# Where the head layouts and the raw keys and queries stand among the loads of an attention and feed-forward kernel

## The chip, the cores and the metric

The kernel runs on one core of one Trainium2 chip. The time is device time in microseconds (us) of one execution. Runs of the same kernel are compared on the same chip; the kernel before has a median of 1001.68 us over 3 runs.

## The reference

Attention with pooled queries, and a feed-forward layer on its output, in float32:

```python
# q, k, v: (4, 8, 1152, 64); 32 heads in all
q_pool = q.reshape(B, H, S // 2, 2, D).mean(axis=3)
scores = scale * np.matmul(q_pool, k.transpose(0, 1, 3, 2))
scores = scores - np.max(scores, axis=-1, keepdims=True)
attn = np.exp(scores)
attn = attn / (np.sum(attn, axis=-1, keepdims=True) + 1e-09)
o = np.matmul(attn, v)
...
h = x @ w_in              # x: (2304, 512), w_in: (512, 2048)
r = np.maximum(h, 0.0)
g = s * (r * r) + b
return g @ w_out          # w_out: (2048, 512)
```

## The kernel before

Products that need more than one pass of a reduced format are split: a number is kept as a high part and the rest, and a product is summed from up to three matmuls. The 32 heads go in 16 pairs. A head takes 9 **steps**, one for each 128 keys, so a pair takes 18; `n` counts the steps and `n % 18` is the step of a pair. In a step TensorE (PE) makes the scores of one block (L486, four matmuls), the products of the block of three steps before with the values (`value_step`, L518 to L528), and one or two matmuls (L456) for the row maxima of a head that comes 15 steps later. ScalarE (ACT) makes the exponentials, VectorE (DVE) the maxima and part of the rests `pl`, GpSimd (POOL) the other rests `pl` (L501) and the preparation. After the attention (from about 585 us) the feed-forward part runs; the change does not touch it. In the last pairs of the attention, weights are converted too.

What is moved or waited for, by its step in a pair:

- `load_v` at steps 3 and 12 (L363): the values of the next head, 288 KB, into one of two buffers `vf`. Step 3 loads for the pair's second head.
- `prep_v` at steps 7 and 16 (L214, L431): POOL makes the high part `vv` and the rest `vl` out of `vf`. PE needs those of the second head from step 12 on.
- `load_k` and `load_q` at step `LR` (L350, L358): the raw keys and queries of the pair three ahead, 4 and 8 DMAs, in pieces of 128 bytes.
- the preparation of the pair two ahead, steps 9 to 14 (table `PREP`): POOL adds the queries (`qs`, L412), DVE transposes, POOL makes high parts and rests (`kh`, `kT`, `qh`, `qz`, `qT`).
- `lay(0)` and `lay(1)`, the entries `l0` and `l1` of `PREP` (L404 to L407): five DMAs inside the on-chip memory that put one prepared head into one of three buffers `kk`/`qq`, 1296 KB. The head is scored 14 steps or more later.
- `shift` (L468 to L472): once a head's maxima are done, DVE reduces them to `c`, and ACT sends `c` into `qq` by two small DMAs. For a pair's second head this is at the end of its step 2, for the first head of the next pair at the end of step 12.
- `xd<-xo` (L567) at step 10: a finished pair goes out.

All these but `c` are issued by SyncE (SP), in the order of the program. The framework gives each DMA of SP and of ACT one of eight completion counters in turn (`DMAHW0` to `DMAHW7`), in the order in which it lists the instructions of all engines. A DMA is issued only once the DMA that had its counter before has landed; the rows of the built program show this as a wait for `DMAHW`. In that list SP's DMAs stand later than the steps that call them, so a `c` that ACT sends can have a counter ahead of a DMA of SP that was called several steps before it.

The lines that decide the place:

```python
if p + 2 < NPAIR and n % 18 == PREP[0][1]:
    prep = prep_pair(p + 2)
for name, at in PREP if n >= 8 else ():
    if n % 18 == at and name in prep:
        prep.pop(name)()
if p + 2 < NPAIR:
    if n % 18 == LR and p + 3 < NPAIR:
        load_k(p + 3)
        load_q(p + 3)
```

Of the kernel before, what the change touches and what calls it, by code (L numbers as in the profile page):

```python
# [34 lines left out]
KIND = "vgvwvgvgw" * 2  # L35

PP = (("ka", 0), ("kb", 0), ("ha", 0), ("hb", 1), ("qs", 1), ("qt", 1), ("qm", 2), ("qh", 2), ("qz", 2), ("kl", 2), ("ql", 3), ("l0", 7))
PREP = (("qs", 9), ("ka", 10), ("kb", 11), ("ha", 11), ("qt", 12), ("hb", 12), ("kl", 12), ("qm", 13), ("qh", 13), ("qz", 13), ("ql", 14), ("l0", 0), ("l1", 8))
LR = 13
LD = 1  # L40
VS = (7, 16)
XT = (1, 2, 3, 4, 8)
# [10 lines left out]
def f32(ap):  # L53
    return ap.bitcast(F32)
# [3 lines left out]
def attention_moe_kernel(ctx: ExitStack, tc: tile.TileContext, q, k, v, w_in, w_out, s_in, b_in, out):  # L58
# [12 lines left out]
    NPAIR = NH // 2  # L71
# [138 lines left out]
    def hi_of(eng, out, in_):  # L210
        if eng is nc.scalar:
            nc.scalar.activation(out, in_, AF.Copy)  # L212
        else:
            eng.tensor_scalar(out=out, in0=in_, scalar1=1.0, scalar2=0.0, op0=ALU.mult, op1=ALU.add)  # L214
# [10 lines left out]
    def tick():  # L225
        step[0] += 1
        due = sorted(x for x in queue if x[0] <= step[0])
        queue[:] = [x for x in queue if x[0] > step[0]]
        for _, _, fn in due:
            fn()  # L230
# [99 lines left out]
    qm = ap.tile([P, P], F32R, name="qm")  # L330
# [16 lines left out]
    def load_k(p):  # L347
        kraw[p] = ap.tile([P, NB, 32], F32, tag="kraw", name=f"kraw{p}")
        for r, b, h, c in quarters(p):
            nc.sync.dma_start(kraw[p][r], k[b, h, :, c].rearrange("(j t) i -> t j i", t=32))  # L350
# [11 lines left out]
    def load_v(hd):  # L362
        nc.sync.dma_start(vfs[hd % 2][:, :, 0:D], v[hd // H, hd % H].rearrange("(j p) d -> p j d", p=P))  # L363

    def prep_pair(p):

        kr, qr = kraw.pop(p), qraw.pop(p)
        kT = ap.tile([P, S], F32, tag="kT", bufs=2, name=f"kT{p}")
        qT = ap.tile([P, SQ], F32, tag="qT", bufs=2, name=f"qT{p}")
        qs = ap.tile([P, NBQ, 32], F32, tag="qs", name=f"qs{p}")  # L370
        kh = ap.tile([P, S], F32R, tag="kh", bufs=2, name=f"kh{p}")
        qh = ap.tile([P, SQ], F32R, tag="qh", bufs=2, name=f"qh{p}")
        krv = kr.rearrange("p j i -> p (j i)")
        lo, hi = slice(0, SQ), slice(SQ, S)

        def corner():
            assert holds.get("qm", -1) == p - 1
            for h in range(2):
                d = slice(h * D, (h + 1) * D)
                hi_of(nc.scalar, qm[d, d], qT[d, NT4 * P:])  # L380
            holds["qm"] = p

        def k_hi(part, last):
            hi_of(nc.scalar if p < 2 else nc.gpsimd, kh[:, part], kT[:, part])
            if last:
                khs[p] = kh

        def q_hi():
            hi_of(nc.scalar if p < 2 else nc.gpsimd, qh, qT)
            qhs[p] = qh  # L390

        def q_blocks():

            for h in range(2):
                r = slice(h * D, (h + 1) * D)
                hi_of(nc.scalar if p < 2 else nc.gpsimd, qzs[p % 2][r, h].rearrange("p (t m) -> p t m", t=NT4), qT[r, :NT4 * P].rearrange("p (m t) -> p t m", t=NT4))

        def lay(h):
            hd = 2 * p + h
            kk, qq = kks[hd % 3], qqs[hd % 3].rearrange("p i a n -> p i (a n)")  # L400
            r = slice(h * D, (h + 1) * D)
            ks = ((f32(kk[D:P, 0, :]), kT[r]), (f32(kk[0:D]), f32(kh[r]).unsqueeze(1).to_broadcast([D, 2, S])))
            for dst, src in ks[::-1] if hd == 0 else ks:
                nc.sync.dma_start(dst, src)  # L404
            nc.sync.dma_start(f32(qq[0:D, 0, :]), f32(qh[r]))
            nc.sync.dma_start(f32(qq[D:P, 0, :]), f32(qh[r]))
            nc.sync.dma_start(f32(qq[0:D, 1, :]), qT[r])  # L407
            holds["k", hd % 3] = hd

        return {  # L410
            "ka": lambda: nc.vector.transpose(out=kT[:, lo], in_=krv[:, lo]),
            "qs": lambda: (nc.vector if p < 2 else nc.gpsimd).tensor_tensor(out=qs, in0=qr[:, :, 0, :], in1=qr[:, :, 1, :], op=ALU.add),  # L412
            "kb": lambda: nc.vector.transpose(out=kT[:, hi], in_=krv[:, hi]),
            "ha": lambda: k_hi(lo, False),
            "qt": lambda: nc.vector.transpose(out=qT, in_=qs.rearrange("p j i -> p (j i)")),
            "hb": lambda: k_hi(hi, True),
            "qh": q_hi,
            "qz": q_blocks,
            "kl": lambda: nc.gpsimd.tensor_tensor(out=kT, in0=kT, in1=f32(kh), op=ALU.subtract),  # L419
            "ql": lambda: nc.gpsimd.tensor_tensor(out=qT, in0=qT, in1=f32(qh), op=ALU.subtract),  # L420
            "qm": corner,
            "l0": lambda: lay(0),
            "l1": lambda: lay(1),
        }
# [55 lines left out]
    def score_step(hd, j, kind):  # L480
        assert holds["k", hd % 3] == holds["c", hd % 3] == hd
        kk, qq = kks[hd % 3], qqs[hd % 3]
        ps = ps_s.tile([P, 2, 512], F32, tag="s", name=f"s{hd}_{j}")
        for a in range(2):
            for i in range(2):
                nc.tensor.matmul(ps[:, a, :HALF], kk[:, i, j * P:(j + 1) * P], qq[:, i, a], start=(i == 0), stop=(i == 1))  # L486
        if kind != "v":
            pe = late.tile([P, 2, HALF], F32, tag="pe", bufs=PE, name=f"pe{hd}_{j}")
        if kind == "w":
            nc.scalar.activation(pe, ps[:, :, :HALF], AF.Exp, scale=SCALE)  # L490
            prob[hd, j] = pe, None
            return
        ph = late.tile([P, 2, HALF], F32R, tag="ph", bufs=PB, name=f"ph{hd}_{j}")
        pl = late.tile([P, 2, HALF], F32R, tag="pl", bufs=PB, name=f"pl{hd}_{j}")
        nc.scalar.activation(ph, ps[:, :, :HALF], AF.Exp, scale=SCALE)  # L495

        full = ps[:, :, :HALF] if kind == "v" else pe
        nc.scalar.activation(full, ps[:, :, :HALF], AF.Exp, scale=SCALE)  # L498
        prob[hd, j] = ph, pl
        eng = nc.vector if kind == "v" else nc.gpsimd  # L500
        fresh.append(lambda: eng.tensor_tensor(out=pl, in0=full, in1=f32(ph), op=ALU.subtract))  # L501
# [92 lines left out]
    prep = prep_pair(0)  # L594
# [11 lines left out]
    for n in range(AHEAD):  # L606
# [3 lines left out]
        if n == 11:  # L610
            load_v(1)
            prep = prep_pair(1)
    nc.sync.dma_start(sb[:, 0:1], s_in.unsqueeze(0).to_broadcast([P, 1]))
    nc.sync.dma_start(sb[:, 1:2], b_in.unsqueeze(0).to_broadcast([P, 1]))

    moe = Moe()
    weights_a = conversions(wa, wstage, 0, SW[0], 1, STA)
    NS = NH * NJ

    for n in range(NS + LAG):  # L620
        hd, j = divmod(n, NJ)

        at = (n - LAG) % NJ if n >= LAG else None
        products = None
        units = iter(range((n + AHEAD) * NU // 18, (n + AHEAD + 1) * NU // 18) if n + AHEAD < NS else ())
        for part in ORD[at] if at is not None else "sff":
            if part == "s" and n < NS:
                score_step(hd, j, KIND[n % 18])
            elif part == "f":
                for u in units:  # L630
                    max_unit(u, ps_m, "m")
                    break
            elif part == "v":
                if products is None:
                    products = value_step(*divmod(n - LAG, NJ))
                next(products)
        for fn in fresh:
            fn()
        fresh.clear()
        if n < NS:  # L640
            p, h = divmod(hd, 2)
            for name, at in PP:
                if n == at:
                    prep.pop(name)()
            if n == LD:
                load_k(2)
                load_q(2)
            if p + 2 < NPAIR and n % 18 == PREP[0][1]:
                prep = prep_pair(p + 2)
            for name, at in PREP if n >= 8 else ():  # L650
                if n % 18 == at and name in prep:
                    prep.pop(name)()
            if p + 2 < NPAIR:
                if n % 18 == LR and p + 3 < NPAIR:
                    load_k(p + 3)
                    load_q(p + 3)
            if hd + 1 < NH:
                if j == LAG and hd >= 1:
                    load_v(hd + 1)
                if n % 18 in VS:  # L660
                    prep_v(hd + 1)
            if n == NS - 3 * NJ:
                moe.fetch(0)
            if n == NS - 2 * NJ:
                moe.split(0, 1)
            if (CB - n) % CP == 0 and 0 <= CB - n < 7 * CP:
                weights_a()
        tick()
# [79 lines left out]
```

## Time and profile before

| | us |
|---|---|
| median of 3 runs | 1001.68 (998.31 to 1002.51) |
| profiled execution, its own time | 1000.3 |
| span in the profile | 998.4 |
| PE busy in the span | 921.4 (92%) |
| DVE, ACT, POOL busy | 630.1, 564.7, 549.8 |

The span is the time from the first to the last instruction in the profile; the 1.9 us around it belong to the execution's own time. PE is the busiest engine, and a busy PE is modelled from its starts, so what the kernel loses is read from PE's idle time and from what ended it.

### The profile page before, as it was taken

Reading aid. Unit: us, or ns where it says so; the run is one execution under the profiler, and the core shown is the slowest. Engines: PE = TensorE matmul, PEld = TensorE weight load, DVE = VectorE, ACT = ScalarE, POOL = GpSimd, SP = SyncE. Lnnn points to the kernel's source line nnn. Section 1 sums busy time; section 2 is a strip of 40 time slices with the busy share of each in tenths; the row PEclk is TensorE's granted clock in tenths of the full one; section 3 lists DMA queues with packets and bytes.
Section 4 is the critical chain, followed back from the end, with each engine's and each line's share of the span. In section 5 each row is a group of like instructions: output and inputs, shape, how many; then the busy total and the mean of one; then the engine's idle time right before and its main releaser. Section 6 shows DMA issues by size and latency. Waiting matters only on the chain.

```text
span 998.4 us, 16537 instructions
## 1 busy us (share of the span) xinstructions
PE 921.4 (92%) x5776; PEld 821.1 (82%) x5776; DVE 630.1 (63%) x1168; ACT 564.7 (57%) x1086; POOL 549.8 (55%) x437
## 2 busy tenths in 40 slices
PE   5998988899899899888889998999999999999998
PEld 3887877788788788877778887789999899999997
DVE  5766776676676668668767556676767664334333
ACT  2776665666676667667667856564444443333332
POOL 7667647757755785786695766673534440010000
PEclk9999999999999999999999999999999999999999
DMA  8987865865686597578574135665354433222311
GB/s 151 174 160 138 173 130 94 175 146 105 131 169 129 103 192 162 108 155 179 108 165 118 46 110 166 201 218 163 127 169 127 148 106 106 64 67 89 99 43 43
DMA packets 255313, 131.18 MB, mean 131 GB/s; under 512 B 203776, under 2 KB 227328, under 8 KB 255232
## 3 DMA queue, kind: packets, MB, share of 16 engines
q1 hardware_dynamic: 244512, 129.62, 54.4%
q10 hardware_dynamic: 10720, 0.52, 0.7%
q8 instruction: 46, 0.75, 0.3%
q14 instruction: 35, 0.29, 0.1%
HBM read 68.68 MB, written 18.87 MB: 88 GB/s over the span
## 4 chain that ended last, share of the span: by engine, by line
PE 58%; POOL 13%; DMA 8%; ACT 8%; DVE 6%; issue 4%; ACTq 1%; SPq 0%; POOLq 0%; DVEq 0%
PE h L272 16%; PE y L299 16%; PE s L486 9%; PE o L524 4%; PE m L456 4%; POOL pl L501 4%; PE o L528 4%; PE o L526 3%; PE o L518 3%; POOL kT L419 2%; POOL qz L214 2%; DMA vf<-in_v_dram 2%; DMA kk<-kh 2%; ACT ph L495 2%; DMA wsto<-in_moe_w_out_dram 2%
## 5 line engine op out<-in xcount | busy, mean ns | idle before, releaser
L457 DVE TENSOR_REDUCE pm<-m 128x1 f32<-128x384 f32 x432 | 233.0, 550 | 128.8 <-PE m L456 124.6
L495 ACT ACTIVATE ph<-s 128x576 fp32r<-128x576 f32 x224 | 145.9, 651 | 133.7 <-PE s L486 114.1
L272 PE MATMUL h<-x,wih 128*128 128x256 f32 x1152 | 213.2, 283 | 6.2 <-DVE gl L286 3.9
L486 PE MATMUL s<-qq,kk 128*128 128x288 f32 x1152 | 213.8, 308 | 4.1 <-DVE pl L501 3.6
L272 PEld LDWEIGHTS h<-x,wih 128*128 128x128 f32 x1152 | 185.8, 189 | 21.2 <-DVE gl L286 3.5
L501 POOL TENSOR_TENSOR pl<-pe,ph 128x576 fp32r<-128x576 f32 x96 | 137.5, 1432 | 104.8 <-ACT pe L498 103.5
L486 PEld LDWEIGHTS s<-qq,kk 128*128 128x128 f32 x1152 | 174.7, 192 | 16.4 <-PE o L528 4.4
L272 PE MATMUL h<-x,wil 128*128 128x256 f32 x576 | 162.2, 282 | 0.0
L528 PE MATMUL o<-pl,vv 128*128 128x288 f32 x448 | 135.7, 303 | 27.4 <-POOL pl L501 27.4
L456 PE MATMUL m<-kh,qz 128*128 128x384 f32 x384 | 153.5, 409 | 5.9 <-DVE pm L457 5.8
L524 PE MATMUL o<-ph,vv 128*128 128x288 f32 x448 | 138.7, 310 | 12.0 <-issue 4.4
L253 POOL TENSOR_TENSOR x<-xr,x 128x1024 fp32r<-128x1024 f32 x27 | 64.8, 2401 | 152.6 <-ACT x L212 146.9
L280 DVE SCALAR_TENSOR_TENSOR h<-h,sb,r 128x256 f32<-128x256 f32 x144 | 70.2, 488 | 115.2 <-ACT r L289 115.2
L526 PE MATMUL o<-ph,vl 128*64 128x288 f32 x448 | 134.1, 299 | 5.4 <-POOL vl L431 5.2
L528 PEld LDWEIGHTS o<-pl,vv 128*128 128x128 f32 x448 | 85.7, 191 | 45.9 <-POOL pl L501 35.4
L289 ACT ACTIVATE r<-h 128x256 f32<-128x256 f32 x144 | 55.7, 387 | 111.0 <-PE h L272 111.0
L501 DVE TENSOR_TENSOR pl<-s,ph 128x576 fp32r<-128x576 f32 x128 | 96.3, 752 | 28.5 <-ACT s L498 21.3
L299 PE MATMUL y<-wol,gh 128*128 128x512 f32 x288 | 113.1, 393 | 0.0
L299 PE MATMUL y<-woh,gl 128*128 128x512 f32 x288 | 112.9, 392 | 0.0
L299 PE MATMUL y<-woh,gh 128*128 128x512 f32 x288 | 112.6, 391 | 0.0
L272 PEld LDWEIGHTS h<-x,wil 128*128 128x128 f32 x576 | 109.6, 190 | 0.0
L524 PEld LDWEIGHTS o<-ph,vv 128*128 128x128 f32 x448 | 85.6, 191 | 25.1 <-ACT l L545 8.0
(89 smaller groups left out, 1492.0 us busy)
## 6 DMA issues: line engine op xcount, KB each, us to landing
kk<-kh SPq DMA_DIRECT2D x32, 576.0 KB, 5.6
kraw<-in_k_dram SPq DMA_DIRECT2D x64, 144.0 KB, 3.7
vf<-in_v_dram SPq DMA_DIRECT2D x32, 288.0 KB, 4.8
kk<-kT SPq DMA_DIRECT2D x32, 288.0 KB, 3.3
qq<-qh SPq DMA_DIRECT2D x64, 144.0 KB, 5.6
xr<-xd SPq DMA_DIRECT2D x18, 512.0 KB, 4.0
qraw<-in_q_dram SPq DMA_DIRECT2D x122, 72.0 KB, 2.5
wsti<-in_moe_w_in_dram SPq DMA_DIRECT2D x16, 512.0 KB, 5.0
```

The lines of the kernel that those rows point to most:

```text
L253: nc.gpsimd.tensor_tensor(out=xl, in0=xr, in1=f32(xh), op=ALU.subtract)
L272: nc.tensor.matmul(h[:, :TB], st[:, c, :], mv[:, c, :], start=(n == 0), stop=(n == 3 * NC - 1))
L280: nc.vector.scalar_tensor_tensor(out=t, in0=h[:, :TB], scalar=sb[:, 0:1], in1=r, op0=ALU.mult, op1=ALU.mult)
L299: nc.tensor.matmul(y[:, :DM], st[:, ts_], mv, start=(first and n == 0), stop=(last and n == 2))
L456: nc.tensor.matmul(ps[:, :KB], st, khs[p][:, e * KB:(e + 1) * KB], start=True, stop=True)
L457: nc.vector.tensor_reduce(out=pms[p][:, col, e:e + 1], in_=ps[:, :KB], axis=AX.X, op=ALU.max)
L486: nc.tensor.matmul(ps[:, a, :HALF], kk[:, i, j * P:(j + 1) * P], qq[:, i, a], start=(i == 0), stop=(i == 1))
L495: nc.scalar.activation(ph, ps[:, :, :HALF], AF.Exp, scale=SCALE)
L501: fresh.append(lambda: eng.tensor_tensor(out=pl, in0=full, in1=f32(ph), op=ALU.subtract))
L524: nc.tensor.matmul(o[:, :HALF], vv[:, j], ph[:, a], start=first, stop=False)
L526: nc.tensor.matmul(o[0:D, :HALF], vl[:, j], ph[:, a], start=False, stop=False)
L528: nc.tensor.matmul(o[:, :HALF], vv[:, j], pl[:, a], start=False, stop=last)
```

## The change

`l0` goes from step 0 of a pair to step 4, behind the value load of step 3; `l1` from step 8 to step 13, behind the value load of step 12; the raw keys and queries from step 13 to step 14, behind `l1`. So that `l1` can be called after `prep` has been replaced at step 9, the two entries are kept in a dictionary of their own, `lays`. The first pair's `l0` (table `PP`) stays.

```diff
-PREP = (("qs", 9), ("ka", 10), ("kb", 11), ("ha", 11), ("qt", 12), ("hb", 12), ("kl", 12), ("qm", 13), ("qh", 13), ("qz", 13), ("ql", 14), ("l0", 0), ("l1", 8))
-LR = 13
+PREP = (("qs", 9), ("ka", 10), ("kb", 11), ("ha", 11), ("qt", 12), ("hb", 12), ("kl", 12), ("qm", 13), ("qh", 13), ("qz", 13), ("ql", 14), ("l0", 4), ("l1", 13))
+LR = 14
...
+    lays = {}
...
-            if p + 2 < NPAIR and n % 18 == PREP[0][1]:
-                prep = prep_pair(p + 2)
-            for name, at in PREP if n >= 8 else ():
-                if n % 18 == at and name in prep:
-                    prep.pop(name)()
+            if n % 18 == PREP[0][1]:
+                lays = {k: prep[k] for k in ("l0", "l1") if k in prep}
+                prep = prep_pair(p + 2) if p + 2 < NPAIR else {}
+            for name, at in PREP:
+
+                ops = prep if name not in ("l0", "l1") or at < PREP[0][1] else lays
+                if n % 18 == at and name in ops and n >= 8:
+                    ops.pop(name)()
```

The first place is SP around the value load of step 3 (`vf1`), in the pair that scores heads 6 and 7. Before, from the fourth query DMA on (the number behind a name is that of a buffer; a wait for `DMAHWn` is one for the DMA that had counter n before):

```order
L358 DMA qraw5_1460<-in_q_dram 32x18x32 [waits DMAHW6_49]
L358 DMA qraw5_1460<-in_q_dram 32x18x32 [waits DMAHW7_49]
L358 DMA qraw5_1460<-in_q_dram 32x18x32 [waits DMAHW0_49]
L358 DMA qraw5_1460<-in_q_dram 32x18x32 [waits DMAHW1_49]
L358 DMA qraw5_1460<-in_q_dram 32x18x32 [waits DMAHW2_49]
L404 DMA kk2_96<-kT4_1348 64x1152 [waits DMAHW3_49,PE_49,Pool_49]
L404 DMA kk2_96<-kh4_1351 64x2x1152 [waits DMAHW4_49,PE_49]
L405 DMA qq2_99<-qh4_1352 64x576 [waits DMAHW5_49,Pool_49]
L406 DMA qq2_99<-qh4_1352 64x576 [waits DMAHW6_49]
L407 DMA qq2_99<-qT4_1349 64x576 [waits DMAHW7_49,Pool_49]
L363 DMA vf1_104<-in_v_dram 128x9x64 [waits DMAHW0_49,PE_49]
L404 DMA kk0_94<-kT4_1348 64x1152 [waits DMAHW1_49,PE_49]
```

Of these waits, the one for counter 0 in the third row and the one for counter 2 in the fifth (the sixth and the eighth query DMA) are waits for the two DMAs of `c7`, head 7's maxima. ACT sends `c7` at the end of step 2 of this pair; the query DMAs were called in step 13 of the pair before. In the changed kernel, from the fourth query DMA on:

```order
L358 DMA qraw5_1484<-in_q_dram 32x18x32 [waits DMAHW6_49]
L358 DMA qraw5_1484<-in_q_dram 32x18x32 [waits DMAHW7_49]
L358 DMA qraw5_1484<-in_q_dram 32x18x32 [waits DMAHW0_49]
L358 DMA qraw5_1484<-in_q_dram 32x18x32 [waits DMAHW1_49]
L358 DMA qraw5_1484<-in_q_dram 32x18x32 [waits DMAHW2_49]
L363 DMA vf1_104<-in_v_dram 128x9x64 [waits DMAHW3_49,PE_49]
L404 DMA kk2_96<-kT4_1343 64x1152 [waits DMAHW4_49,Pool_49]
L404 DMA kk2_96<-kh4_1346 64x2x1152 [waits DMAHW5_49]
L405 DMA qq2_99<-qh4_1347 64x576 [waits DMAHW6_49,Pool_49]
L406 DMA qq2_99<-qh4_1347 64x576 [waits DMAHW0_49]
```

Now `c7` has the counters 6 and 0, so the fourth and the sixth query DMA wait for it; the value load stands right behind the queries, and the five DMAs of `l0` behind it, without a wait for PE.

The second place is SP from the value load of step 12 (`vf0`) to the keys, in the pair that scores heads 4 and 5. Before:

```order
L404 DMA kk1_95<-kT3_921 64x1152 [waits DMAHW4_49,PE_49]
L404 DMA kk1_95<-kh3_924 64x2x1152 [waits DMAHW5_49,PE_49]
L405 DMA qq1_98<-qh3_925 64x576 [waits DMAHW6_49]
L406 DMA qq1_98<-qh3_925 64x576 [waits DMAHW0_49]
L407 DMA qq1_98<-qT3_922 64x576 [waits DMAHW1_49]
L567 DMA xd0_72<-xo1_1263 128x576 [waits DMAHW3_49,Pool_49]
L363 DMA vf0_103<-in_v_dram 128x9x64 [waits DMAHW4_49,PE_49]
L350 DMA kraw5_1455<-in_k_dram 32x36x32 [waits DMAHW5_49,DVE_49]
L350 DMA kraw5_1455<-in_k_dram 32x36x32 [waits DMAHW6_49]
L350 DMA kraw5_1455<-in_k_dram 32x36x32 [waits DMAHW7_49]
L350 DMA kraw5_1455<-in_k_dram 32x36x32 [waits DMAHW1_49]
```

The wait for counter 7, of the third key DMA, is the one for `c6` (head 6, sent at the end of step 12). In the changed kernel:

```order
L567 DMA xd0_72<-xo1_1263 128x576 [waits DMAHW6_49,Pool_49]
L363 DMA vf0_103<-in_v_dram 128x9x64 [waits DMAHW7_49,PE_49]
L404 DMA kk1_95<-kT3_916 64x1152 [waits DMAHW0_49]
L404 DMA kk1_95<-kh3_919 64x2x1152 [waits DMAHW1_49]
L405 DMA qq1_98<-qh3_920 64x576 [waits DMAHW2_49]
L406 DMA qq1_98<-qh3_920 64x576 [waits DMAHW3_49]
L407 DMA qq1_98<-qT3_917 64x576 [waits DMAHW4_49]
L350 DMA kraw5_1479<-in_k_dram 32x36x32 [waits DMAHW5_49,DVE_49]
L350 DMA kraw5_1479<-in_k_dram 32x36x32 [waits DMAHW7_49]
L350 DMA kraw5_1479<-in_k_dram 32x36x32 [waits DMAHW1_49]
L350 DMA kraw5_1479<-in_k_dram 32x36x32 [waits DMAHW2_49]
```

`l1` now stands between the value load and the keys. `c6` has the counters 2 and 5, so the third DMA of `l1` and the first key DMA wait for it. PE, ACT, DVE and POOL have the same work in the same order as before, but for the counters.

## Rows read from the trace of the kernel before

**Rows 1.** PE's waits, 70 to 350 us: total us, times, longest.

```profile
PE o L528 <- POOL pl L501: 18.3, 16, 1.6
PE o L526 <- POOL vl L431: 5.2, 6, 0.9
PE o L524 <- POOL vv L214: 4.0, 5, 1.5
```

**Rows 2.** PE's waits, 350 to 530 us.

```profile
PE o L528 <- POOL pl L501: 9.1, 7, 2.4
```

**Rows 3.** POOL's waits, 70 to 530 us.

```profile
POOL vv L214 <- DMA vf<-in_v_dram: 60.0, 13, 6.4
```

**Rows 4.** POOL in order of time: start, us, what, [idle before].

```profile
141.77 1.43 POOL L501 TENSOR_TENSOR pl<-pe,ph 128x576 fp32r<-128x576 f32 x1 [0.54 <-ACT pe L498]
149.57 0.67 POOL L214 TENSOR_SCALAR vv<-vf 128x576 fp32r<-128x576 f32 x1 [6.37 <-DMA vf<-in_v_dram]
...
161.46 1.40 POOL L501 TENSOR_TENSOR pl<-pe,ph 128x576 fp32r<-128x576 f32 x1
```

**Rows 5.** PE in order of time, the same stretch.

```profile
150.30 0.40 PE L524 MATMUL o<-ph,vv 128*128 128x288 f32 x1 [1.54 <-POOL vv L214]
...
151.78 0.35 PE L526 MATMUL o<-ph,vl 128*64 128x288 f32 x1 [0.91 <-POOL vl L431]
...
154.52 0.40 PE L528 MATMUL o<-pl,vv 128*128 128x288 f32 x1 [0.89 <-POOL pl L501]
...
162.91 0.40 PE L528 MATMUL o<-pl,vv 128*128 128x288 f32 x1 [1.61 <-POOL pl L501]
163.15 0.30 PE L524 MATMUL o<-ph,vv 128*128 128x288 f32 x1
```

**Rows 6.** SP in order of time: start, us over the group, what, count.

```profile
117.92 5.77 SPq L350 DMA_DIRECT2D kraw<-in_k_dram  x4
...
136.77 0.47 SPq L404 DMA_DIRECT2D kk<-kT  x1
...
142.48 0.61 SPq L363 DMA_DIRECT2D vf<-in_v_dram  x1
...
145.23 0.90 SPq L405 DMA_DIRECT2D qq<-qh  x1
...
149.66 0.60 SPq L567 DMA_DIRECT2D xd<-xo  x1
```

**Rows 7.** SP's own waits, 70 to 530 us.

```profile
SPq L358 <- DMA qq<-c: 119.0, 13, 11.5
```

**Rows 8.** ACT's issues of `c` (steps 2, 12, 2); landing of the first and second.

```profile
133.37 0.49 ACTq L471 DMA_DIRECT2D qq<-c  x1
...
151.71 0.49 ACTq L471 DMA_DIRECT2D qq<-c  x1
...
169.56 0.49 ACTq L471 DMA_DIRECT2D qq<-c  x1
...
qq<-c ACTq DMA_DIRECT2D x1, 2.0 KB, 1.9
...
qq<-c ACTq DMA_DIRECT2D x1, 2.0 KB, 4.7
```

**Rows 9.** Value loads to landing; query DMAs, ns each, and landing of five.

```profile
DMA to landing us min/median/max: 3.1/4.8/7.0
...
L358 SPq DMA_DIRECT2D qraw<-in_q_dram x122: 311/496/1522, 5.4 to 489.8; - x122
...
qraw<-in_q_dram SPq DMA_DIRECT2D x5, 72.0 KB, 2.4
```

**Rows 10.** A window: us, busy us of PE, PEld, DVE, ACT, POOL, PE's granted clock, DMA share, GB/s.

```profile
222.10:225.30 3.20, 3.03 (x13) 2.48 (x13) 2.09 (x3) 1.70 (x4) 3.12 (x5) 0.50 1.07 251
```

**Rows 11.** Windows of eight pairs and of the next five, columns as in Rows 10.

```profile
70.35:350.23 279.88, 248.96 (x1594) 221.94 (x1593) 191.05 (x345) 184.00 (x337) 187.42 (x154) 0.99 0.69 137
350.23:529.76 179.53, 161.21 (x1002) 142.18 (x1001) 130.82 (x234) 121.78 (x224) 132.62 (x109) 0.98 0.72 150
```

## The prediction

> **What bounds the kernel now.** I looked first for the idle time of the busiest engine. In the attention PE is busy 248.96 of 279.88 us over eight pairs (35.0 us a pair) and 161.21 of 179.53 us over the five pairs in which weights are converted as well (35.9 us a pair); DVE, ACT and POOL are each far less busy [rows 11]. So an unhindered PE would set the pace, and what the pairs lose is in PE's waits. Over the eight pairs it waits 18.3 us for rests `pl`, 5.2 us for `vl` and 4.0 us for `vv`, 27.5 us in all; over the five, 9.1 us for `pl` [rows 1, 2]. All of these POOL makes.
>
> The second view is POOL's own waits: it sits idle 60.0 us in 13 pairs, 4.6 us a pair, for the values `vf` [rows 3]. POOL works in order, so this one wait delays all that is queued behind it. In one pair it is done with the rest of step 7 at 143.20 us (141.77 and 1.43), waits 6.37 us, and begins `vv` at 149.57; the rest of step 14, 11.9 us of POOL's work later, begins at 161.46 and PE takes it at 162.91 [rows 4, 5]. PE's four waits of that pair (1.54, 0.91, 0.89, 1.61) hang on the one load [rows 5].
>
> The third view, SP in order of time, tells why the load is late. It was called at step 3 but issued at 142.48, after the keys, the queries and `l0`, which alone holds SP from 136.77 to 142.48, 5.7 us [rows 6]. And the queries did not go out as fast as SP could: SP waits 119.0 us, in 13 pairs, with a query DMA for the landing of a `c`, 9.2 us each [rows 7]. The rows of the built program, in the section on the change, show why: the sixth query DMA has a counter that the `c` of step 2 had before it. In this pair ACT sends `c` at 133.37, and it lands 1.9 us later [rows 8]. I call 133.37 the pair's zero: `c` lands at 1.9, the load is issued at 9.1, `vv` begins at 16.2, and POOL was free for it at 9.8.
>
> **The change, part by part.** It removes no work and adds none: the same DMAs, the same instructions on every engine.
>
> *Behind the wait.* Before, three queries (0.5 us each [rows 9]) and `l0` (5.7 us) stood between the landing of `c` and the load: 7.2 us. Now the fourth query has `c`'s counter, so five queries stand there, 2.5 us, and `l0` comes after the load. The load is issued at 4.4 if `c` lands in 1.9 us, at 7.2 if it lands in 4.7, as the one of step 12 does with keys in flight [rows 8]. Value loads take 3.1 to 7.0 us to land, 4.8 in the median [rows 9]. Today a layout stands ahead of the load; then it is queries, which land in 2.4 us [rows 9]. I bound the landing by 3.1 and by 3.1 + 2.4 = 5.5, and take 4.0. The values are there at 4.4 + 3.1 = 7.5 at best and at 7.2 + 5.5 = 12.7 at worst; with `c` landing in 3.3 us, midway since keys will be draining, at 5.8 + 4.0 = 9.8. POOL is free at 9.8 too. So POOL's wait goes nearly to nothing. A rule of the Trainium skill speaks against it: by "DMA: Bandwidth & Descriptors" ("Specifications") pieces under 512 bytes miss the line rate, and the load now stands behind five DMAs of 128-byte pieces. By the rule the load would land at the late end, and the sum would be that of the first rival below; no run here shows yet what a load behind queries takes.
>
> *Does the wait of PE go with it?* PE reaches the rest of step 14 at 162.91; without its four waits, and 0.1 us for each restart (a first product takes 0.40 us and not 0.30), it would be there at 162.91 - 4.95 - 0.4 = 157.6 [rows 5]. POOL, begun at 143.20, has that rest done 11.9 + 1.40 us later, at 156.5 [rows 4]. That is 1.1 us in hand: the wait can go, but a POOL that begins over 1 us late makes PE wait again.
>
> *The moved layouts.* `l0` now follows the load, and `l1` the load of step 12. Neither waits for PE any more, since the buffer is long free. They are needed 14 steps later, some 27 us at 1.9 us a step, for a few us of transfer: nothing. If that cover were gone, scores would wait.
>
> *The raw keys and queries* go behind `l1`, and they wait for `c` of step 12 with `l1`'s third DMA. From that `c`, sent at 151.71, to the next at 169.56 there are 17.8 us, of which the two later waits of PE take 2.7; in 15.1 us SP gets 4.7 for the landing, 4.4 for the rest of `l1` (145.23 to 149.66), 5.8 for the keys and 1.5 for three queries: 16.4 [rows 5, 6, 8]. The next `c` then lands at 15.1 + 1.9 to 4.7, so SP is ready 0.6 to 3.4 us before it. It fits, but not by much. POOL adds the queries only behind `vv` and `vl`, so not before 9.8 + 0.67; the last ones are issued by 7.2 and land 2.4 us later.
>
> *The sum.* PE's waits on POOL: 27.5 + 9.1 = 36.6 us in 34 waits [rows 1, 2], and 3.4 us of restarts, 40.0. Off that: a POOL that begins late now and then, which I put at 0.5 us of PE in each of 13 pairs, 6.5; and half of the 9.1 in the five pairs with weights, where POOL has 26.5 us of work a pair and not 23.4 [rows 11], 4.6. On to that: the clock. In a window of 3.2 us the granted clock is 0.50, that is 1.2 GHz instead of 2.4 [rows 10], and the mean over the two stretches is 0.99 and 0.98 [rows 11]: up to 0.01 x 279.88 + 0.02 x 179.53 = 6.4 us, if it fell for PE's waits. I take 2.4, since the means are rounded and the cause is open. "TensorE: Matmul & The Clock Gate" of the Trainium skill ("The HAM clock gate") calls the throttled state the default, which activity releases; by it all 6.4 would come back if the waits go, and the sum would be 4.0 lower.
>
> 40.0 - 6.5 - 4.6 + 2.4 = 31.3 us. The profiled execution took 1000.3 us, so I predict 969.0. That execution lies 1.4 us under the median, 1001.68, which changes nothing here.
>
> **The rivals.**
>
> *The load stays late (0.12).* `c` lands among the keys in 4.7 us and the load behind the queries takes 5.5: the values are there at 12.7 and POOL waits 2.9 us a pair instead of 4.6. For it speaks the rule above, and that SP reaches the fourth query only just in time; against it, that a longer pair gives SP the time back. It leaves 37% of 40.0, 14.8 us: 985.5.
>
> *POOL's second half becomes the bound (0.13).* The load comes in time, but the 1.1 us in hand are eaten by work that today hides in the wait: half of the 18.3 us and all of the 9.1 for `pl` stay, 18.3, with 1.5 of restarts. Then 40.0 - 19.8 = 20.2: 980.1. For it speaks that POOL's 11.9 us have no idle time between them.
>
> *Slower (0.03).* The raw loads behind `l1` overrun. SP must be ready for the fourth query before `c` lands; each us beyond the 0.6 to 3.4 in hand makes the values later, and from 16.2, instead of 9.8, the load is later than before. So it decides from an overrun of 6.4 us on top of the margin; one of 7.8 us would cost 1.4 us in 13 pairs, 18: 1018. The rest of `l1` and the keys take 4.4 and 5.8 us today [rows 6], and they would have to take nearly double.
>
> *No change that shows (0.03).* PE's waits go, but the maxima or the exponentials take their place. DVE and ACT are busy 68% and 66% [rows 11], so this needs a queue that I don't see: 998.
>
> **How the numbers follow.** My forecast has the remaining 0.69. Its own range is 956 to 980: the low end is all of the 40.0 and most of the clock, the high end doubles the two terms that I took off. With the first two rivals 0.94 lies on the faster side. Leaving out the slow cases and the tail of the late load, 80% is 955 to 984. The measurement can tell about 0.5%, 5 us, from no change: faster by more 0.94, within it 0.03, slower 0.03.
>
> **What the profile after would show.** SP: the load of step 3 right behind the eight queries, 4.4 to 7.2 us after `c`, and `l0` behind it; the wait of the queries for `c` still there, but shorter. POOL: `vv<-vf` waits at most 10 us in place of 60. PE: no waits for `vv` and `vl`, those for `pl` under 13 us over both stretches, and a pair of about 32 us. I am wrong if POOL's wait stays over 30 us, if `pl` waits stay with POOL never idle, or if scores wait for `kk` or `qq`.

## The result, and the profile after

The changed kernel takes 990.5 us in the median (989.04 to 991.4, 4 runs), the kernel before 1000.86 beside it (998.31 to 1002.51, 4 runs): a ratio of 0.9897, 95% interval 0.9871 to 0.9923. It is faster by 10.4 us, where 31 were forecast, and lies outside the range of 955 to 984. The profiled execution took 989.98 us, its span is 988.0.

The waits show first that the predicted thing happened. POOL's wait for the values, from 70 to 515 us (total us, times, longest):

```profile
POOL vv L214 <- DMA vf<-in_v_dram: 2.8, 5, 0.8
```

This was 60.0 us in 13 pairs [rows 3]. SP in order of time, in the pair of [rows 6], and POOL under it:

```profile
134.95 2.48 SPq L358 DMA_DIRECT2D qraw<-in_q_dram  x5
137.52 0.44 SPq L363 DMA_DIRECT2D vf<-in_v_dram  x1
138.06 0.77 SPq L404 DMA_DIRECT2D kk<-kT  x1
...
147.75 0.38 SPq L363 DMA_DIRECT2D vf<-in_v_dram  x1
148.18 0.60 SPq L404 DMA_DIRECT2D kk<-kT  x1
148.83 0.62 SPq L404 DMA_DIRECT2D kk<-kh  x1
```

```profile
142.85 0.67 POOL L214 TENSOR_SCALAR vv<-vf 128x576 fp32r<-128x576 f32 x1
143.60 1.44 POOL L431 TENSOR_TENSOR vl<-vf,vv 128x576 fp32r<-128x576 f32 x1
```

The load goes out right behind the queries and ahead of `l0`, at 137.52 instead of 142.48 [rows 6], and POOL begins `vv` without a wait, at 142.85 instead of 149.57 [rows 4]. PE's waits in eight pairs (68 to 345 us), and in the five behind them (345 to 515):

```profile
PE s L486 <- DVE pl L501: 16.5, 8, 2.3
...
PE o L528 <- POOL pl L501: 1.9, 4, 0.6
```

The first row is from the eight pairs, the second from the five. PE's waits for POOL's rests and values are nearly gone: 27.5 and 9.1 us before [rows 1, 2], 0.4 and 1.9 now. But in each of the eight pairs PE now waits about 2 us, with the next scores `s`, for a rest `pl` that DVE makes. One such wait, followed back: PE, then DVE, then ACT, each in order of time:

```profile
150.12 0.81 PE L486 MATMUL s<-qq,kk 128*128 128x288 f32 x4
...
153.26 0.29 PE L528 MATMUL o<-pl,vv 128*128 128x288 f32 x1
155.50 0.77 PE L486 MATMUL s<-qq,kk 128*128 128x288 f32 x4 [1.94 <-DVE pl L501]
```

```profile
150.22 0.17 DVE L468 TENSOR_REDUCE c<-pm 128x5 fp32r<-128x15 f32 x1
...
151.27 0.56 DVE L457 TENSOR_REDUCE pm<-m 128x1 f32<-128x384 f32 x1 [0.19 <-PE m L456]
154.60 0.76 DVE L501 TENSOR_TENSOR pl<-s,ph 128x576 fp32r<-128x576 f32 x1 [2.77 <-ACT s L498]
```

```profile
149.41 0.65 ACT L490 ACTIVATE pe<-s 128x576 f32<-128x576 f32 x1
150.42 0.49 ACTq L471 DMA_DIRECT2D qq<-c  x1
151.00 2.32 ACTq L472 DMA_DIRECT2D qq<-c  x1
153.37 0.65 ACT L495 ACTIVATE ph<-s 128x576 fp32r<-128x576 f32 x1 [3.31 <-PE m L456]
153.92 0.65 ACT L498 ACTIVATE s<-s 128x576 f32<-128x576 f32 x1
```

DVE is not busy; it waits 2.77 us for ACT. ACT is not busy either. Its exponential at 153.37 shows a wait of 3.31 us put down to PE, but the scores that it reads were done at 150.93 (L486, 150.12 and 0.81). What stands directly ahead of it is ACT's own queue: 0.4 us until DVE has made `c`, 0.5 for the first DMA of the step-12 `c`, and 2.32 us in which the second (L472) is being issued. Just ahead, at 148.18 and 148.83, SP has issued the two large DMAs of `l1`. That line over 68 to 345 us (duration in ns, minimum, median and maximum), before and then after:

```profile
L472 ACTq DMA_DIRECT2D qq<-c x16: 474/613/1027, 81.8 to 344.3; - x16
```

```profile
L472 ACTq DMA_DIRECT2D qq<-c x16: 613/1448/2692, 82.3 to 337.7; - x16
```

In the changed kernel the eight of step 12 take 2.28 to 2.69 us each, the eight of step 2, which have no layout ahead of them, 0.61. No counter holds the eight: the DMAs that each of them has to wait for, by the counters, had landed 9.4 us or more before its issue began. SP's own rows have the same hold, before the change too. The fourth DMA of a layout, the second small one behind the two large ones (L406), before and then after:

```profile
138.84 2.64 SPq L406 DMA_DIRECT2D qq<-qh  x1
...
146.18 2.57 SPq L406 DMA_DIRECT2D qq<-qh  x1
```

```profile
140.45 2.66 SPq L406 DMA_DIRECT2D qq<-qh  x1
```

Before, it took 2.43 to 2.69 us in all sixteen layouts of the eight pairs. In the changed kernel it takes 2.44 to 2.78 in `l0` and 0.60 in `l1`, where the two DMAs of `c` go out between the large ones and SP's small ones. The hold has gone from SP, where no exponential stood behind it, to ACT.

The last thing to read is the clock. Windows of the eight pairs, the five, the pair behind them and a short one behind one of the waits (columns as in [rows 10]):

```profile
70.84:343.58 272.74, 251.84 (x1594) 225.75 (x1593) 189.48 (x345) 183.74 (x336) 188.24 (x153) 0.98 0.68 140
343.58:515.45 171.87, 158.44 (x1003) 139.40 (x1002) 133.52 (x234) 121.66 (x225) 134.94 (x109) 1.00 0.73 156
515.45:551.88 36.43, 31.99 (x197) 28.63 (x196) 22.53 (x39) 24.95 (x45) 20.68 (x16) 0.95 0.40 105
120.90:124.30 3.40, 3.40 (x12) 2.83 (x12) 1.61 (x3) 1.61 (x3) 2.77 (x2) 0.50 0.44 103
```

Over the eight pairs PE's idle time fell from 30.92 to 20.90 us, and its busy time rose by 2.9, against [rows 11], so that 7.1 us are gained. In the window at 120.90 the granted clock is 0.50, that is 1.2 GHz; PE had waited 2.15 us just before it. The same comes behind waits of 2.31, 2.26 and 2.13 us; the others, of 1.9 to 2.0 us, have none behind them. (The length of the wait doesn't decide it alone: in the run below with the two DMAs of `c` in the other order, a clock of 0.50 stands behind waits of 1.79, 1.86 and 1.99 us, and none behind one of 2.13.) The five pairs gain 7.7 us. The pair behind them loses 3.6 (32.85 us before): it has the new wait, 2.13 us, and a slow clock behind it. That makes 11.2 us; the rest of the span gives 0.8 of them back, and 10.4 remain.

### The profile page after: what moved, and what is told of

The parts are those of the page before. It is cut to its first block, busy times and chain, and to the rows that moved or that the text cites. A ratio compares the mean times of both kernels' runs of the same rounds, so it can differ in the third digit from the quotient of the medians.

```text
span 988.0 us, 16507 instructions
## 1 busy us (share of the span) xinstructions
PE 921.8 (93%) x5776; PEld 822.9 (83%) x5776; DVE 631.3 (64%) x1168; ACT 564.2 (57%) x1086; POOL 552.7 (56%) x437
## 4 chain that ended last, share of the span: by engine, by line
PE 63%; DVE 9%; ACT 9%; POOL 6%; DMA 6%; issue 3%; ACTq 3%; SPq 1%; DVEq 0%; POOLq 0%
PE h L272 18%; PE y L299 17%; PE s L486 10%; PE m L456 4%; PE o L524 4%; PE o L528 4%; PE o L526 3%; PE o L518 3%; DVE pm L457 2%; ACT ph L495 2%; DVE pl L501 2%; ACTq L472 2%; DMA wsto<-in_moe_w_out_dram 2%; ACT s L498 2%; POOL pl L501 2%
## 5 line engine op out<-in xcount | busy, mean ns | idle before, releaser
L486 PE MATMUL s<-qq,kk 128*128 128x288 f32 x1152 | 215.6, 310 | 24.9 <-DVE pl L501 24.2
L486 PEld LDWEIGHTS s<-qq,kk 128*128 128x128 f32 x1152 | 174.5, 192 | 40.7 <-issue 23.7
L528 PE MATMUL o<-pl,vv 128*128 128x288 f32 x448 | 133.1, 297 | 1.9 <-POOL pl L501 1.9
L501 DVE TENSOR_TENSOR pl<-s,ph 128x576 fp32r<-128x576 f32 x128 | 96.2, 751 | 50.7 <-ACT s L498 49.0
L283 ACT ACTIVATE gh<-h,sb 128x256 fp32r<-128x256 f32 x144 | 68.1, 473 | 64.6 <-DVE h L280 64.3
```

What stands on the lines that cost most here:

```text
L283: nc.scalar.activation(gh, t, AF.Identity, bias=sb[:, 1:2])
L528: nc.tensor.matmul(o[:, :HALF], vv[:, j], pl[:, a], start=False, stop=last)
```

## The experiments

**Theory A**: the two large DMAs of `l1`, which SP now issues just ahead of the step-12 `c`, hold ACT's second DMA of that `c`, and with it the exponentials, DVE's rest and PE. **Theory B**: DVE's transposes crowd together at steps 10 to 12, and DVE is late by itself. The first four kernels ran beside a median before of 1000.62 us, the next four beside 1000.51, the last two beside 1001.53; the kernel before differs by 1 us between the groups, so kernels of different groups are compared by their times. "Wait" is PE's wait for `pl` from DVE from 68 to 345 us, 16.5 us in the changed kernel.

**Only `l0` moved.** `l1` is back at step 8:

```diff
-... ("l0", 4), ("l1", 13))
-LR = 14
+... ("l0", 4), ("l1", 8))
+LR = 13
```

> The layout of the first head at step 4 as in the change, that of the second back at step 8 and the raw loads at step 13. Theory A (the second layout's two large DMAs, issued just ahead of the step-12 maxima c, hold ACT's second c DMA for 2.3 us, so that exponentials, DVE's rests and then PE come late): here the layout is issued several us before c, ACT's second c DMA takes 0.6 us again, PE's wait for DVE's pl (16.5 us in eight pairs) goes under 3 us, and the time is 965 to 972 us. Theory B (with POOL no longer waiting, DVE's transposes fall together at steps 10 to 12 and make its rests late): the wait of PE stays as in the changed kernel and the time is 988 to 993 us.

971.01 us, ratio 0.9708 (0.9687 to 0.9728). One half of the change is thus worth 29.6 us, and the other half takes 19.5 of them back.

```profile
PE s L486 <- DVE pl L501: 3.7, 9, 0.9
...
L472 ACTq DMA_DIRECT2D qq<-c x17: 558/613/1273, 80.9 to 335.4; - x17
```

No second DMA takes over 1.27 us, the wait falls to 3.7 (A had under 3), and from 34 us to the last microsecond no stretch has a clock of 0.50. DVE's transposes are at the same steps as in the changed kernel. B falls.

**Only `l1` moved.** `l0` is back at step 0:

```diff
-... ("l0", 4), ("l1", 13))
+... ("l0", 0), ("l1", 13))
```

> The layout of the second head at step 13 and the raw loads at 14 as in the change, that of the first head back at step 0, ahead of the value load of step 3. Both theories: POOL waits for the values again, 50 to 65 us in 13 pairs, so the gain is gone. Theory A: ACT's c DMA is held where the layout is close ahead of it, which adds up to 1 us a pair: 1000 to 1010 us. Theory B: POOL is late as in the kernel before, so DVE is not crowded: 998 to 1002 us.

994.4 us, ratio 0.994 (0.992 to 0.996): faster, where both theories had no change or a loss, so A missed here too. POOL still waits 50.7 us for the values, and ACT's second DMA is held 2.22 to 2.53 us at each step-12 `c`. But PE's wait for DVE is 9.7 us and not 16.5. Over both stretches it is 17.8 instead of 2.0 before, and the waits for POOL's rests are 10.3 instead of 27.4. The two do not add up: while PE stands for DVE, POOL catches up, and the wait that would have come next is gone. That is how I read the rows; no run tested it.

**The `c` of the first head two steps later**, everything else as changed:

```diff
-        later(1, send)
+        later(1 if h else 3, send)
```

> The changed kernel with the maxima c of a pair's first head sent two steps later (end of step 14 and not 12), the second head's as before. Theory A: by then the layout's large DMAs have been worked off for 3 us more, the hold on ACT falls below 1 us, PE's wait for DVE's pl falls under 5 us in eight pairs, and the time is 966 to 976 us. Theory B: 988 to 993 us, since DVE's work does not move.

962.22 us, ratio 0.9622 (0.9602 to 0.9642), the fastest kernel here that does all the work, and a little under A's range. There is no wait for DVE left in the eight pairs, and the mean clock is 0.998. Windows of its eight and five pairs:

```profile
70.03:320.55 250.52, 245.94 (x1594) 221.86 (x1593) 189.31 (x345) 183.80 (x336) 188.39 (x153) 1.00 0.75 152
320.55:490.92 170.37, 157.90 (x1003) 139.45 (x1002) 132.00 (x234) 121.65 (x225) 134.17 (x109) 1.00 0.74 157
```

The second DMA of those `c` still takes 0.97 to 1.68 us, and PE does not wait for it. ACT shows why:

```profile
145.59 0.49 ACTq L471 DMA_DIRECT2D qq<-c  x1
145.79 0.65 ACT L495 ACTIVATE ph<-s 128x576 fp32r<-128x576 f32 x1
146.12 1.35 ACTq L472 DMA_DIRECT2D qq<-c  x1
146.34 0.65 ACT L498 ACTIVATE pe<-s 128x576 f32<-128x576 f32 x1
147.57 0.65 ACT L495 ACTIVATE ph<-s 128x576 fp32r<-128x576 f32 x1 [0.58 <-PE s L486]
```

Exponentials still run while the DMA is being issued, so that ACT sits idle for 0.28 to 0.93 us ahead of the next one, and not for 3.27 to 3.68 as in the changed kernel. The fourth DMA of `l1` is SP's again, and takes 2.43 to 2.67 us there.

**One DMA of the `c` left out.** The first head of each pair but the first pair doesn't get its second DMA, so the maxima of its last 64 queries aren't updated:

```diff
+            if h or hd < 2:
                 nc.scalar.dma_start(f32(row[D:D + 1, NT4 * P:]), ...)
```

> The changed kernel without the second of the two c DMAs of each pair's first head (but the very first): the maxima of the last 64 query rows of these heads are not brought up to date, all other work stays. Theory A: nothing is left on ACT to be held but the first c DMA, which was not held (0.49 us), so PE's wait for DVE's pl falls under 3 us in eight pairs: 965 to 972 us. Theory B: 988 to 993 us.

961.0 us, ratio 0.9607 (0.959 to 0.9624), 4 us under A's range. `l1` is where the change put it, the first DMA of that `c` is issued where it was, and the wait is gone. So the 29.5 us between this kernel and the changed one hang on that DMA of 64 words a pair: on its hold and on the half microsecond that it takes without one. (With one DMA fewer, the counters of all the later ones shift too.)

**The later `c` alone**, in the kernel before (the edit of one line above):

> The kernel before with one edit: the first head's c is sent two steps later; no layout and no load is moved. Theory A (the two large DMAs of l1 just ahead of the c of step 12 hold ACT's second DMA): nothing stands just ahead of that c here, so nothing is gained: 995 to 1004 us, POOL still waits 55 to 65 us for the values, and PE still waits 25 us or more for pl from POOL. Rival C (a later c is better by itself, with or without the moved layouts): 985 to 992, in the kernel before too.

1000.45 us, ratio 1.0006 (0.9994 to 1.0017); POOL waits 60.6 us for the values, PE 26.5 us for `pl`. The later `c` has no worth of its own here.

**The `c` one step later** instead of two:

```diff
-        later(1, send)
+        later(1 if h else 2, send)
```

> The changed kernel, with the first head's c sent one step later instead of two. Theory A: the two large DMAs of l1 have about 1.9 us more to drain before ACT's second DMA, which was held 2.3 us and stays near the 1.0 to 1.7 us that were seen two steps later: PE waits for pl from DVE below 8 us over the eight pairs, 961 to 972 us. Rival C (what counts is which step the c falls into, where the exponentials have time in hand, and not the distance to l1): the hold stays over 2 us and the time lies at 975 to 990, or the wait stays and only moves.

964.03 us, ratio 0.9645 (0.9622 to 0.9667). The time is A's. The hold lies between A's (1.0 to 1.7) and C's (over 2): 1.46 to 2.31 us at those `c`. And PE does not wait for DVE's `pl` at all.

```profile
L472 ACTq DMA_DIRECT2D qq<-c x17: 613/1462/2311, 82.1 to 333.7; - x17
```

ACT's idle time ahead of the next exponential is 0.58 to 1.42 us here. As I read these rows, the hold alone isn't the loss; it needs an ACT that has run out of work ahead of the `c`, and an exponential behind it for which DVE and PE have no time in hand.

**`l1` behind the `c`**, as I thought, by calling it and the raw loads at step 15:

```diff
-... ("l1", 13))
-LR = 14
+... ("l1", 15))
+LR = 15
```

> The changed kernel with l1 at step 15 and the raw keys and queries behind it at step 15: l1 is now behind the c of step 12, and the c itself is where it was. Theory A: ACT's second DMA of that c takes 0.5 to 0.9 us as before, the waits of PE for pl from DVE stay under 5 us over the eight pairs, no clock of 0.50 in them, 957 to 968 us; SP comes about 2 us later to the query that waits for the c of step 2, so POOL may wait up to 15 us for the values. Rival C (the c at its old step is what hurts): as the changed kernel, 985 to 992. Rival D (SP comes too late to the load of step 3): POOL waits over 25 us for the values and the time is 970 to 985.

989.07 us, ratio 0.9889 (0.9874 to 0.9903). A's number missed, since the edit did not do what it was made for. SP had nothing to wait for between the value load and `l1`, and issued it at once, ahead of the `c` as before:

```profile
145.54 0.60 SPq L404 DMA_DIRECT2D kk<-kT  x1
146.19 0.62 SPq L404 DMA_DIRECT2D kk<-kh  x1
```

```profile
147.78 0.49 ACTq L471 DMA_DIRECT2D qq<-c  x1
148.37 2.21 ACTq L472 DMA_DIRECT2D qq<-c  x1
150.62 0.65 ACT L495 ACTIVATE ph<-s 128x576 fp32r<-128x576 f32 x1 [3.20 <-PE o L524]
```

The run is the change once more: same order of issue, same hold, same time. It says nothing on C.

**Only `l0` moved, and the later `c`:**

> Only l0 moved (l1 back at step 8, raw loads at step 13), and the first head's c sent two steps later. Theory A: nothing large stands ahead of the c in either place, so about as l0 alone, 971: 966 to 973 us. Rival C: a further gain like that in the changed kernel, to 955 to 963.

965.42 us, ratio 0.9653 (0.9639 to 0.9667), between the two ranges. No `c` is held long in either kernel (up to 1.27 us in `l0` alone, 1.10 here), and yet the `c` at its old step cost the 5.6 us by which this one beats `l0` alone; PE's 3.7 us of waits for DVE are gone with it. So C has a share, though a small one.

**The small DMAs of a layout first.** The largest of `l1`, 576 KB, then waits for the first DMA of the step-12 `c`, and the `c` keeps its step:

```diff
-            for dst, src in ks[::-1] if hd == 0 else ks:
-                nc.sync.dma_start(dst, src)
             nc.sync.dma_start(f32(qq[0:D, 0, :]), f32(qh[r]))
             nc.sync.dma_start(f32(qq[D:P, 0, :]), f32(qh[r]))
             nc.sync.dma_start(f32(qq[0:D, 1, :]), qT[r])
+            for dst, src in ks[::-1] if hd == 0 else ks:
+                nc.sync.dma_start(dst, src)
```

> The changed kernel, with the five DMAs of each layout in another order: the three small ones (queries) first, the two large ones (keys) behind them, so that the largest of l1, 576 KB, waits for the first DMA of the step-12 c and can no longer be in flight ahead of it; the c keeps its step. Theory A: ACT's second DMA of that c is held 0.6 to 1.5 us and no longer 2.3 to 2.7, PE's waits for pl from DVE over the eight pairs fall from 16.5 to below 9 us, no clock of 0.50 behind them, 962 to 976 us. Rival C (the c at its old step is what hurts, whatever is in flight): the wait stays at about 2 us in each pair, 985 to 992.

972.51 us, ratio 0.9725 (0.9694 to 0.9756). Same DMAs, same steps, another order of five, and 18 us are back:

```profile
PE s L486 <- DVE pl L501: 6.8, 9, 1.3
...
L472 ACTq DMA_DIRECT2D qq<-c x17: 474/614/1647, 82.5 to 340.6; - x17
```

**The two DMAs of the `c` in the other order**, the one of 64 words first (L471), the one of 512 second (L472):

> The changed kernel, with ACT's two DMAs of a c in the other order, the one of 64 words first and the one of 512 words second. Theory A, in the form that whatever ACT issues behind the two large DMAs is held until they have drained: the two DMAs together still take 2.5 us or more of ACT at the step-12 c, and the time stays at 985 to 993. Rival F (what is held is only a DMA behind the one of 512 words, since that one is not yet taken up): both issue in about 0.5 to 0.7 us, the waits of PE fall below 6 us over the eight pairs, 962 to 973.

988.49 us, ratio 0.9868 (0.9827 to 0.9909): as A had it.

```profile
114.48 0.47 ACTq L471 DMA_DIRECT2D qq<-c  x1
114.99 2.55 ACTq L472 DMA_DIRECT2D qq<-c  x1
117.59 0.65 ACT L495 ACTIVATE ph<-s 128x576 fp32r<-128x576 f32 x1 [3.47 <-PE m L456]
```

The first of the two goes out in half a microsecond and the second is held, whichever it is; the size of the one ahead doesn't matter. F falls.

Put together, for a `c` at its old step: the mean time that the second DMA takes to issue, and PE's wait for each (the waits over their count).

| kernel | second DMA, us | PE's wait, us | time, us |
|---|---|---|---|
| `l0` alone | 0.79 | 0.41 (3.7 / 9) | 971.0 |
| small DMAs first | 1.12 | 0.76 (6.8 / 9) | 972.5 |
| other order of the `c` | 2.38 | 1.94 (15.5 / 8) | 988.5 |
| the change | 2.45 | 2.06 (16.5 / 8) | 990.5 |

The wait is the issue time less 0.4 us in all four rows. From the second row to the third the time grows by 16 us and these waits by only 8.7; the five pairs behind add 1.9 (2.7 instead of 0.8), and in the last two kernels the clock falls as well, to a mean of 0.991 and 0.990 over the span, against 0.996 and 0.998 in the first two. The first two rows have `c` at its old step, and give back 18.0 to 19.5 of the 28.3 us between the change and the later `c`: that much hangs on what stands ahead of the `c`. The rest came back only with a later `c`, or without its second DMA.

## Why the prediction was wrong

**What bounds the kernel, and *Behind the wait*: right.** Zero is 133.05 here: the load was issued 4.5 us after it (4.4 to 7.2 were given), and the value loads of step 3 land in 3.8 to 4.7 us, 4.2 in the median (4.0 was taken). Before, behind `l0`, they took 3.6 to 7.0, 4.4 in the median; the 4.8 of [rows 9] has those of step 12 in it. So no late end shows behind the queries' small pieces, against what I made of the Trainium skill's "DMA: Bandwidth & Descriptors" ("Specifications"). The rival "the load stays late" falls.

***Does the wait of PE go with it?* Right.** It went: 0.4 us for POOL's `pl` in eight pairs. It is 0.2 us with the later `c`, so it isn't PE's new wait that gives POOL the time. The 1.1 us in hand held, and the rival "POOL's second half" falls.

***The raw keys and queries*: right.** SP still waits for the `c` with a query, 70.6 us in 13 pairs instead of 119.0 [rows 7], so it is there in time, and with 5.4 us in hand on average, not 0.6 to 3.4.

***The moved layouts*: the step that failed.** I asked who needs `l0` and `l1`, found 27 us of cover, and wrote "nothing". I didn't ask whom they hinder. The rows of the built program showed `l1`'s two large DMAs between the value load and the DMA that waits for `c6`; I read that wait from SP's side alone, and never what `c6` would find ahead of it, nor what stands behind `c6` on ACT: the exponentials. The size of the hold stood in the profile before: 2.64 of the 5.7 us that `l0` kept SP, which I used as a price of SP's time, were the one small DMA at 138.84. I didn't ask which of the five took them, and so not what the same place in the order would cost on ACT. The price, by the runs: between 18 us (990.5 less 972.5, the small DMAs first) and 28 us (990.5 less 962.2, which has C's share in it). The rival "no change that shows" named the thing, the exponentials in place of POOL, but gave it 0.03 and saw no queue for it.

***The sum*: near, for the part that it covered.** The later `c` takes the failed step away and leaves all the others: 1000.6 less 962.2 is 38.4 us, against 31.3, within the forecast's own range of 956 to 980. The 6.5 us for a late POOL were too much: in that kernel PE waits 0.2 us for POOL's `pl` in the eight pairs. The half of the five pairs' 9.1 us that I kept is about right: 4.4 us remain. The clock's 2.4 should have been some 4. Two pairs of before, the first with a stretch at 0.50 in it, the second without:

```profile
210.02:245.42 35.40, 32.29 (x201) 28.75 (x200) 24.04 (x44) 22.99 (x42) 23.44 (x21) 0.95 0.71 142
245.42:281.17 35.75, 30.91 (x201) 27.60 (x200) 23.93 (x44) 22.98 (x42) 23.41 (x20) 1.00 0.67 133
```

PE is busy 1.4 us longer in the first, and 1.2 to 1.4 in the two such pairs among the five: 4.0 us, and all of it came back, since both stretches are at 1.00 with the later `c`. Busy time fell by 6.3 us in all, from 248.96 to 245.94 and from 161.21 to 157.90 [rows 11]; that has the restarts in it, which the sum had counted already. "TensorE: Matmul & The Clock Gate" of the Trainium skill ("The HAM clock gate") calls the throttled state the default, which activity releases. The trace agrees so far: with the waits gone no stretch at 0.50 is left, and in the changed kernel the four between 70 and 560 us all stand at or behind the new waits. The 6.4 us that I worked out by it were too much, since the means were rounded.

## What to carry to other kernels

Before a large transfer is moved, list what other engines issue just behind its new place, and what work is queued behind that issue. Read the issue times of the transfers that are already there, on whatever engine: a long one can move with the order. A transfer with ample time can hold up a tiny one on another engine, and the compute instructions behind it. When a compute engine seems to wait for something that was long done, look one row up in its own queue for a DMA with an issue time over its usual one. A call at a later place in the code doesn't make a queue that waits for nothing issue later; the order within the queue, or a transfer that it must wait for, does.

## What the runs showed of the hardware

An issue of ACT, 0.56 to 0.61 us as a rule, takes 2.2 to 2.7 us when SP has issued 288 and 576 KB of transfers inside the on-chip memory 2 to 3 us before; the first small DMA still goes out in 0.49, the second is held. It isn't a matter of ACT: an issue of SP in the same place, the second small DMA behind the two large ones, took 2.43 to 2.69 us in the kernel before. "Issuing engines are not separate DMA queues" in the Trainium skill's "DMA: Bandwidth & Descriptors" says that DMAs of all engines run on the same 16 DMA engines, which fits, and that the time to initiate one is "usually small relative to the DMA itself". Here it was not: 2.32 us of issuing, of 4.9 from the start of the issue to the landing. What in the chip holds the second DMA, whether the bytes in flight or the number of pieces, stays open; no run parted the two.
